# Stage 2 of a long convolution: two frequencies on the partition halves, real and imaginary parts side by side

## The chip, the cores and the metric

One core of a Trainium2 chip runs the whole program in one launch. The metric is device time in microseconds (us), as a median over several executions. The engines are TensorE (PE, with its weight loads shown apart as PEld), VectorE (DVE), ScalarE (ACT), GpSimd (POOL) and SyncE (SP), which here only issues DMAs.

## The reference: a filter convolution, then a feed-forward layer

```python
h_mlp = np.maximum(pos_emb @ w1, 0.0) @ w2            # 12480 x 128
h_filt = h_mlp * np.exp(-0.01 * pos)[:, None]
u = x * v                                             # 2 x 12480 x 128
y = irfft(rfft(u, n=2*S) * rfft(h_filt, n=2*S), n=2*S)[:, :S]
a = x * y                                             # then, per token:
h = a @ w_in                                          # 128 -> 2048
out = (h / (1.0 + np.exp(-h))) @ w_out                # 2048 -> 128
```

The two batches are convolved with the same filter, channel by channel. `w_in` and `w_out` are float64 and are converted on the chip.

## The kernel before, in words

A sequence is padded to two blocks (`NI = 2`) of 6272 = 98 x 64 positions. The long transform is done in two steps, both as matmuls with constant matrices: 98 points along t1 (stage 1), and for each of the 98 results k1 another 64 points along t2, with the twiddle factors folded into the matrix (stage 2). The pointwise product of the spectra is done block by block: the first block of the output is u0*h0, the second u0*h1 + u1*h0.

Stage 1 (lines 213 to 412) is written out by hand in the string `P["seq"]`, one letter a step: `x` loads a group of four channels of x and v, `m` and `d` multiply them on GpSimd and VectorE, `A`/`a` transform a group of batch 0 and copy it out of PSUM on ACT or DVE (`stage_a`, 32 groups), `p` loads positions, `Z` makes 8 of 128 columns of the filter's hidden layer (`zeros_block`, 16 times), `H`/`h` transforms a group of four hidden units (16 groups), and `w` is one step of the conversion of a 512-column piece of `w_in` or `w_out` (8 pieces). In `stage_a` the stationary operand is 98 x 128 (both blocks, 64 positions t2 each) and 196 columns are moved (98 real, 98 imaginary), so that the PSUM rows are (block, t2), while the tile `X` wants (real or imaginary, t2) on its rows; four copies of 64 rows a group do that. Batch 0 comes first here, mixed with the filter's `Z` and the weights; the filter's `H` steps stand behind the `|`.

Stage 2 for batch 0 is the loop at line 536: one iteration takes a pair q of k1 (49 pairs). On PE it issues `up` (transform of X, L419), `sp` (second layer of the filter, L555 and L556, on 64 and 128 rows by turns), `hp` (filter transform three pairs ahead, L290) and `wp` (inverse transform two pairs back, L419). Real and imaginary parts lie on the partition halves there, so that a complex product needs copies across halves: `uw` is i times `up` (two ACT copies, L436, L438), `hab` needs both halves twice (two ACT copies, a DMA from one half to the other at L559, a DVE copy at L575), and `zt` takes four copies (L300 to L303 on ACT for odd pairs, L305 to L308 on DVE for even ones). The products are `at` on DVE and `bt` on POOL (L444, L451), their sum on DVE (L457), and the last addition, `pair_v` (L461), on POOL. Each pair loads one `fb` tile (constants), stores `hs` (the filter's spectrum, used again for batch 1) and `wd` (the result).

Stage 3 is the feed-forward layer over 52 token tiles, with the inverse transform along t1 (`yp`, L611) ahead of each tile, and batch 1 carried through stages 1 and 2 in its shadow. It uses the old `stage_a` and the old pair functions and keeps them.

Each engine works through its queue strictly in the order of the program. SP issues the loads and stores in that order, too.

Of the kernel before, what the change touches and what calls it, by code (L numbers as in the profile page):

```python
# [58 lines left out]
def tile_offsets():  # L59
# [8 lines left out]
    late=2,  # L68
    xb=8,
    pb=4,  # L70
    nw1=6,
    wb1=2,
    wb2=1,
    by1=5,
    by2=9,
    seq='wwppwZxwmxZcwmxxxmmwZwxAAmmpZxxapAxAdwwwAxxwxxAZmZAwddwmpmZwwwwxAmaxwwwwxwawxZxwmwAmAddwAwwZmwAxxxdpxwwmmwwAZmawxwaAwwZwAxwdpwxwwwZmwaAxpwwmwawZmwxxxmwwwwxwwdwwwwAwAwwmwZwwZwwwwwwwwwwwwwAawwwwwwwwwwwwmwZAwwwwwwwwAwawwwwww|HwwhwwHwHwhwwxHwhHHhHHxwwhwwwHwHmhmwfffwwwwwwwwwwAwwwAbwbwwwwbw',
# [13 lines left out]
def kernel(  # L90
# [12 lines left out]
    fb: bass.AP,  # L103
    win: bass.AP,
# [13 lines left out]
    hs = dram.tile([NQ, 64, 1024], F32, name="hs")  # L118
# [3 lines left out]
    fa_sb = const.tile([R, 196], F32, name="fa_sb")  # L122
# [4 lines left out]
    w2_sb = const.tile([128, D], F32, name="w2_sb")  # L127

    def weights(wp, src, nm, bufs, dst):
# [15 lines left out]
        t = wp.tile([128, n], U32, name=f"wt{nm}", tag="wt", bufs=bufs)  # L145
        e = wp.tile([128, n], U32, name=f"we{nm}", tag="we", bufs=bufs)
# [27 lines left out]
        nc.sync.dma_start(out=dst, in_=a)  # L174
# [7 lines left out]
    def skewed(gens, by):  # L182

        live = list(enumerate(gens))
        t = 0
        while live:
            for i, g in list(live):
                if t >= by * i:
                    try:
                        next(g)  # L190
                    except StopIteration:
                        live.remove((i, g))
                        continue
# [9 lines left out]
    NLATE = P["late"]  # L203
    xpool = pool("xpool")
    X = xpool.tile([128, R, NI * D], F32, name="X")
    zpool = pool("zpool")
    z = zpool.tile([R, NJ, 128], F32, name="z")
    stg = pool("stg", side="right")
    wprep = pool("wprep", side="right")
    psz = pool("psz", space=PSUM, side="right")  # L210
    psa = pool("psa", space=PSUM)

    def stage_a(psp, lhs, dst, on_act, nm, bufs):

        ap = psp.tile([128, 4, 256], F32, name=f"ap{nm}", tag="ap", bufs=bufs)
        for k in range(4):
            nc.tensor.matmul(ap[:, k, 0:196], lhs(k), fa_sb, start=True, stop=True)  # L217
# [15 lines left out]
    def uv_tiles(b, g, sp):  # L233
        if b == 1:
            return [slot(512 * k)[0:R].rearrange("p (d t) -> p d t", t=128) for k in (g % 4, 4 + g % 4)]
        n = P["xb"] if g < D // 4 - NLATE else NLATE
        return [sp.tile([R, 4, 128], F32, name=f"{t}s{b}_{g}", tag=t, bufs=n) for t in "xv"]
# [31 lines left out]
    def stage_a_group(b, g, psp, us, bufs, on_act):  # L269
        stage_a(  # L270
# [8 lines left out]
    def load_fb(rp, q, bufs, e):  # L279
        t = rp.tile([128, 2, 2, 128], F32, name=f"fb{q}", tag="fb", bufs=bufs)  # L280
        e.dma_start(out=t, in_=fb[q])
        return t
# [3 lines left out]
    def hb_step(q):  # L286

        hp = php.tile([128, 2, 2, 64], F32, name=f"hp{q}", tag="hp", bufs=2)
        for k in range(2):
            nc.tensor.matmul(  # L290
                hp[:, k].rearrange("p c k -> p (c k)"),
                Xh[2 * q >= KA][:, 2 * q - (2 * q >= KA) * KA + k],
                fbs[q][:, k, 0],
                start=True,
                stop=True,
            )
        zt = rpa.tile([128, 2, 4, 64], F32, name=f"zt{q}", tag="zt", bufs=3)
        hf = hp.rearrange("p k c m -> p (k c) m")
        if q % 2:
            nc.scalar.copy(out=zt[64:128, 1], in_=hf[64:128])  # L300
            nc.scalar.copy(out=zt[0:64, 0], in_=hf[0:64])
            nc.scalar.copy(out=zt[0:64, 1, 1:3], in_=hf[0:64, 0:4:3])
            nc.scalar.activation(out=zt[0:64, 1, 0:4:3], in_=hf[0:64, 1:3], func=AF.Copy, scale=-1.0)  # L303
        else:
            nc.vector.tensor_copy(zt[64:128, 1], hf[64:128])  # L305
            nc.vector.tensor_copy(zt[0:64, 0], hf[0:64])
            nc.vector.tensor_copy(zt[0:64, 1, 1:3], hf[0:64, 0:4:3])
            nc.vector.tensor_scalar(  # L308
                out=zt[0:64, 1, 0:4:3], in0=hf[0:64, 1:3], scalar1=-1.0, scalar2=None, op0=ALU.mult
            )  # L310
        zs[q] = zt
# [5 lines left out]
    nc.scalar.dma_start(out=w2_sb[0:64], in_=w2)  # L317
    nc.scalar.dma_start(out=w2_sb[64:128], in_=w2)
    nc.scalar.dma_start(out=fai_sb, in_=fai)

    def w_gen(k):
# [5 lines left out]
        return weights(wprep, src, k, P["wb1"] if k < P["nw1"] else P["wb2"], dst)  # L327
# [15 lines left out]
    def filter_group(g, on_act):  # L343
        stage_a(
            psa,
            lambda k: z[:, 4 * g + k],
            lambda c, i: [
                (h[64 * c : 64 * c + 64, :, i * NJ + 4 * g : i * NJ + 4 * g + 4], k0, k1)
# [4 lines left out]
            3,  # L353
        )
# [3 lines left out]
    w_steps = skewed([w_gen(k) for k in range(P["nw1"])], P["by1"])  # L358
    n_a = n_z = n_h = n_f = 0
    for t in P["seq"]:  # L360
# [6 lines left out]
        elif t in "Aa":  # L367
            stage_a_group(0, n_a, psa, uss.pop(n_a), 3, t == "A")
            n_a += 1
        elif t == "p":  # L370
            g = len(pts)
            pts.append(wprep.tile([128, NP, R], F32, name=f"pt{g}", tag="pt", bufs=P["pb"]))
# [3 lines left out]
        elif t == "Z":  # L376
            zeros_block(n_z)
            n_z += 1
        elif t in "Hh":
# [556 lines left out]
```

## Time and profile before

| | us |
|---|---|
| median of 3 runs (all: 1633.18, 1633.42, 1628.67) | 1633.18 |
| the profiled execution | 1626.7 |
| its span | 1624.7 |
| PE busy in the span | 1591.1 |
| DVE busy | 1285.6 |
| ACT busy | 1108.2 |
| POOL busy | 575.4 |

The profiled execution's time is 2.0 us over its span, which is what lies around it. Stage 1 fills about the first 116 us, stage 2 the next 186, and stage 3 the rest. The share of busy time is a mean over these, so the stages are looked at one by one. A matmul of f32 operands is shown as two passes, each with a weight load.

### The profile page before, as it was taken

To read this page: it belongs to the slowest core of one execution; us is meant where nothing else is said; L and a number is where in the kernel's file an instruction comes from. 1 tells how busy PE (TensorE), PEld (TensorE's weight loads), DVE (VectorE), ACT (ScalarE), POOL (GpSimd) and SP (SyncE) were. 2 spreads that over 40 slices of the span, in tenths; PEclk is the share of its full clock that TensorE was granted. 3 is DMA by queue.
4 is the path that set the end of the run, shared out by engine and by line. 5 is a ranking of instruction groups with operands and counts; after the bars stand their busy time and mean duration, and the time that the engine had idled before them with its cause. 6 is when DMAs were issued, how large, how long until landed. Compare 5 with 4: busy or idle time off the path is not lost.

```text
span 1624.7 us, 27176 instructions
## 1 busy us (share of the span) xinstructions
PE 1591.1 (98%) x9376; PEld 1369.7 (84%) x9376; DVE 1285.6 (79%) x2182; ACT 1108.2 (68%) x2151; POOL 575.4 (35%) x564
## 2 busy tenths in 40 slices
PE   7899999899999999999999999999999999999999
PEld 6787777688888888988888888888888898888888
DVE  5979899765688889888888887777777777777776
ACT  5598898767777777777777775555555555555555
POOL 5627778632156656666666650000000000000000
PEclk9899999889999999999999999999999999999999
DMA  9838999854255554555554541111111111111110
GB/s 264 235 100 229 237 262 259 236 137 121 77 132 138 132 145 128 153 134 148 135 137 133 135 109 53 43 50 49 33 47 48 47 43 38 44 50 47 35 41 18
DMA packets 130001, 186.99 MB, mean 115 GB/s; under 512 B 11346, under 2 KB 79608, under 8 KB 129864
## 3 DMA queue, kind: packets, MB, share of 16 engines
q1 hardware_dynamic: 89480, 147.58, 33.2%
q10 hardware_dynamic: 40384, 37.67, 8.3%
q8 instruction: 75, 1.23, 0.3%
q14 instruction: 62, 0.51, 0.1%
HBM read 125.36 MB, written 53.42 MB: 110 GB/s over the span
## 4 chain that ended last, share of the span: by engine, by line
PE 79%; DMA 1%; issue 0%; SPq 0%; POOL 0%; ACT 0%; DVE 0%; POOLq 0%
PE op L841 12%; PE op L843 11%; PE op L842 11%; PE hq L814 11%; PE hq L813 11%; PE hq L815 11%; PE yp L611 6%; PE wp L419 2%; PE up L419 2%; PE ap L217 2%; DMA slots<-in_v_dram 1%; DMA slots<-wd 0%; POOL slots L245 0%; SPq L240 0%; DVE att L622 0%
## 5 line engine op out<-in xcount | busy, mean ns | idle before, releaser
L820 ACT ACTIVATE g<-hq 128x486 f32<-128x486 f32 (+3 forms) x448 | 255.6, 570 | 224.2 <-PE hq L815 214.3
L825 DVE TENSOR_TENSOR gl<-g,gh 128x486 fp32r<-128x486 f32 (+3 forms) x448 | 294.4, 657 | 94.7 <-PE hq L815 59.4
L841 PE MATMUL op<-gh,woh 128*128 128x490 f32 (+3 forms) x832 | 323.4, 389 | 0.0
L814 PE MATMUL hq<-al,wih 128*128 128x490 f32 (+3 forms) x832 | 315.9, 380 | 0.0
L813 PE MATMUL hq<-ah,wih 128*128 128x490 f32 (+3 forms) x832 | 315.8, 380 | 0.0
L843 PE MATMUL op<-gh,wol 128*128 128x490 f32 (+3 forms) x832 | 315.4, 379 | 0.0
L815 PE MATMUL hq<-ah,wil 128*128 128x490 f32 (+3 forms) x832 | 315.4, 379 | 0.0
L842 PE MATMUL op<-gl,woh 128*128 128x490 f32 (+3 forms) x832 | 315.1, 379 | 0.0
L820 ACT ACTIVATE hq<-hq 128x490 f32<-128x490 f32 (+2 forms) x384 | 214.1, 559 | 93.8 <-PE hq L815 65.6
L825 DVE TENSOR_TENSOR gl<-hq,gh 128x490 fp32r<-128x490 f32 (+2 forms) x384 | 251.7, 662 | 32.6 <-ACT gh L824 22.1
L822 DVE CAST gh<-hq 128x490 fp32r<-128x490 f32 (+2 forms) x288 | 188.9, 656 | 50.0 <-ACT hq L820 48.4
L822 DVE CAST gh<-g 128x486 fp32r<-128x486 f32 (+3 forms) x336 | 137.7, 410 | 56.9 <-ACT g L820 54.9
L813 PEld LDWEIGHTS hq<-ah,wih 128*128 128x128 f32 x832 | 156.7, 188 | 25.6 <-DVE gl L825 0.8
L814 PEld LDWEIGHTS hq<-al,wih 128*128 128x128 f32 x832 | 156.6, 188 | 24.9
L841 PEld LDWEIGHTS op<-gh,woh 128*128 128x128 f32 x832 | 156.5, 188 | 24.9
L815 PEld LDWEIGHTS hq<-ah,wil 128*128 128x128 f32 x832 | 156.7, 188 | 24.6
L843 PEld LDWEIGHTS op<-gh,wol 128*128 128x128 f32 x832 | 156.3, 188 | 25.0
L842 PEld LDWEIGHTS op<-gl,woh 128*128 128x128 f32 x832 | 156.6, 188 | 19.7 <-DVE gl L825 0.3
L223 ACT COPY X<-ap 64x392 f32<-64x392 f32 x208 | 99.8, 480 | 34.4 <-PE ap L217 32.2
L611 PEld LDWEIGHTS yp<-fai_sb,slots 98*64 98x64 f32 x2048 | 89.3, 138 | 17.9 <-issue 16.7
L611 PE MATMUL yp<-fai_sb,slots 98*64 98x98 f32 (+1 forms) x2048 | 99.4, 252 | 0.3 <-DMA slots<-wd 0.3
L623 ACT CAST ah<-att 128x490 fp32r<-128x490 f32 (+3 forms) x52 | 30.9, 594 | 90.5 <-DVE att L622 90.5
(1068 smaller groups left out, 2546.7 us busy)
## 6 DMA issues: line engine op xcount, KB each, us to landing
slots<-hs SPq DMA_DIRECT2D x98, 256.0 KB
slots<-wd SPq DMA_DIRECT2D x48, 490.0 KB
hs<-hab SPq DMA_DIRECT2D x49, 256.0 KB
wd<-ws SPq DMA_DIRECT2D x49, 256.0 KB
slots<-in_fb_dram SPq DMA_DIRECT2D x49, 256.0 KB
wd<-slots ACTq DMA_DIRECT2D x49, 256.0 KB
fb<-in_fb_dram ACTq DMA_DIRECT2D x45, 256.0 KB
xs<-in_x_dram SPq DMA_DIRECT2D x32, 196.0 KB
```

The lines of the kernel that those rows point to most:

```text
L223: nc.scalar.copy(out=o, in_=src[:, k0:k1])
L419: nc.tensor.matmul(out[:, k].rearrange("p i d -> p (i d)"), f[:, k], a[:, k], start=(i == 0), stop=(i == len(passes) - 1),)
L611: nc.tensor.matmul(yp[h : h + 64, o : o + ws[t]], wt[:, c, t * D + h : t * D + h + 64], fai_sb[:, c, 0 : ws[t]], start=(c == 0), stop=(c = ...
L813: nc.tensor.matmul(hp[:, 0:w], wih[:, fs], ah[:, 0:w], start=True, stop=False)
L814: nc.tensor.matmul(hp[:, 0:w], wih[:, fs], al[:, 0:w], start=False, stop=False)
L815: nc.tensor.matmul(hp[:, 0:w], wil[:, fs], ah[:, 0:w], start=False, stop=True)
L820: nc.scalar.activation(out=g[:, 0:w], in_=hp[:, 0:w], func=AF.Silu)
L822: nc.vector.tensor_copy(gh[:, 0:w], g[:, 0:w])
L825: nc.vector.tensor_tensor(out=gl[:, 0:w], in0=g[:, 0:w], in1=gh[:, 0:w].bitcast(F32), op=ALU.subtract)
L841: nc.tensor.matmul(o[:, 0:w], woh[:, fs], gh[:, 0:w], start=(f == 0), stop=False)
L842: nc.tensor.matmul(o[:, 0:w], woh[:, fs], gl[:, 0:w], start=False, stop=False)
L843: nc.tensor.matmul(o[:, 0:w], wol[:, fs], gh[:, 0:w], start=False, stop=(f == NF - 1))
```

## The change

Stage 2 of batch 0 is laid out anew: the two frequencies of a pair lie on the partition halves, and real and imaginary parts side by side in the free dimension. `up`, `sp` and `hp` become four matmuls each, with 64 stationary columns (column halves of the array: k = 0 to PSUM rows 0 to 63, k = 1 to rows 64 to 127); `wp` becomes four matmuls with 64 rows (row halves), each frequency into a PSUM bank of its own. The constants come in a new array `fc` of the same size. `w2_sb` is block-diagonal. What was a copy across halves is now another place in the same row: `zt` is one copy, `hab` one copy and one negated copy of half the size, `us` one copy. `pair_v` goes to DVE in every iteration.

Stage 1 uses `stage_a_halves` for the filter and for batch 0: 64 stationary columns (one block) and 98 moved ones, real parts to the lower, imaginary ones to the upper half of the PSUM rows, so that two copies of 128 rows a group are left of four of 64. For the filter, the second block also gets the first block's share with another constant, added in PSUM (`wrap`, eight matmuls more a group). The string `seq` is new: all `Z`, then all `H`, then the 32 groups of batch 0. `X` now lies where `z`, the positions and the first four weight pieces were; 14 groups of x and v have a buffer (5 of them in `stg1`, whose room the last four weight pieces take after group 4). Weight stores are issued by GpSimd.

```diff
+    def stage_a_halves(psp, lhs, dst, on_act, nm, bufs, wrap=False):
+        ap = psp.tile([128, NI, 512], F32, name=f"ap{nm}", tag="ap", bufs=bufs)
+        for i in range(NI):
+            for k in range(4):
+                for c in range(2):
+                    nc.tensor.matmul(
+                        ap[64 * c : 64 * c + 64, i, k * R : k * R + R],
+                        lhs(k, i),
+                        fa_sb[:, c * R : c * R + R],
+                        start=True,
+                        stop=not (wrap and i),
+                    )
+                for c in range(2 if wrap and i else 0):
+                    nc.tensor.matmul(
+                        ap[64 * c : 64 * c + 64, i, k * R : k * R + R],
+                        lhs(k, 0),
+                        fa_sb[:, (2 + c) * R : (3 + c) * R],
+                        start=False,
+                        stop=True,
+                    )
+        for i in range(NI):
+            src = ap[:, i, 0 : 4 * R].rearrange("p (d k) -> p k d", d=4)
+            for o, k0, k1 in dst(i):
+                if on_act:
+                    nc.scalar.copy(out=o, in_=src[:, k0:k1])
+                else:
+                    nc.vector.tensor_copy(o, src[:, k0:k1])
...
     def hb_step(q):
...
+            for i in range(NI):
+                nc.tensor.matmul(
+                    hp[64 * i : 64 * i + 64, k],
+                    Xh[2 * q >= KA][:, 2 * q - (2 * q >= KA) * KA + k, i * NJ : i * NJ + NJ],
+                    fbs[q][:, 0, k],
+                    start=True,
+                    stop=True,
+                )
+        zs[q] = rpa.tile([128, 2, 2, 64], F32, name=f"zt{q}", tag="zt", bufs=3)
+        nc.scalar.copy(out=zs[q].rearrange("p k c m -> p k (c m)"), in_=hp)
...
         elif t in "Aa":
+            if n_a == 0:
+                for g in w_steps[: P["nw1"]]:
+                    assert next(g, None) is None
+                wprep.release()
+                ppool.release()
+                zpool.release()
+                xpool = pool("xpool")
+                X = xpool.tile([128, R, NI * D], F32, name="X")
             stage_a_group(0, n_a, psa, uss.pop(n_a), 3, t == "A")
             n_a += 1
+            if n_a == P["x1"]:
+                stg1.release()
+                wprep = pool("wprep2", side="right")
+                w_steps += [w_gen(k) for k in range(P["nw1"], 8)]
...
+    def pair_u0(q):
+        up = pp.tile([128, 2, NI, D], F32, name=f"up0_{q}", tag="up", bufs=2)
+        for c in range(2):
+            for k in range(2):
+                nc.tensor.matmul(
+                    up[64 * k : 64 * k + 64, c].rearrange("p i d -> p (i d)"),
+                    fbs[q][:, 0, k, 64 * c : 64 * c + 64],
+                    X[:, 2 * q + k],
+                    start=True,
+                    stop=True,
+                )
+        us = rp.tile([128, 2, NI, D], F32, name=f"us{q}", tag="uw", bufs=2)
+        nc.scalar.copy(out=us, in_=up)
+        return up, us
+
+    def filter_spectrum(q):
+        sp_ = pps.tile([128, 2, 2, D], F32, name=f"sp{q}", tag="sp", bufs=2)
+        zt = zs.pop(q)
+        for c in range(2):
+            for k in range(2):
+                nc.tensor.matmul(
+                    sp_[64 * k : 64 * k + 64, c].rearrange("p s d -> p (s d)"),
+                    zt[:, k, c],
+                    w2_sb,
+                    start=True,
+                    stop=True,
+                )
+        hab = rp.tile([128, 3, 2, D], F32, name=f"hab{q}", tag="hab", bufs=3)
+        nc.scalar.copy(out=hab[:, 1:3], in_=sp_)
+        nc.scalar.activation(out=hab[:, 0], in_=sp_[:, 1], func=AF.Copy, scale=-1.0)
+        return hab
...
+    def last_w(q):
+        wp = pp.tile([128, 2, 512], F32, name=f"wp0_{q}", tag="wp", bufs=1)
+        at, inv = prods.pop(q)[0], fbs.pop(q)[:, 1]
+        for c in range(2):
+            for k in range(2):
+                h = slice(64 * k, 64 * k + 64)
+                nc.tensor.matmul(wp[:, k, 0:256], inv[h, c], at[h, c], start=(c == 0), stop=(c == 1))
+        store_w(0, q, rp, wp[:, :, 0:256], nb)
...
+        if it >= 0:
+            up, us = pair_u0(it)
+        if it >= 1:
+            pair_s(*prods[it - 1])
+        if it + 1 < NQ:
+            habs[it + 1] = filter_spectrum(it + 1)
+        if 3 <= it + 3 < NQ:
+            hb_step(it + 3)
+        if it >= 0:
+            hab = habs.pop(it)
+            at = products(it, up, hab[:, 1:2], "at", 3, nc.vector)
+            bt = products(it, us[:, ::-1], hab[:, 0:3:2], "bt", 2, nc.gpsimd)
+            prods[it] = at, bt
+            nc.sync.dma_start(out=hs[it], in_=hab[:, 1:3].rearrange("p m s d -> p (m s d)"))
+        if it >= 1:
+            pair_v(prods[it - 1][0], nc.vector)
+        if it >= 2:
+            last_w(it - 2)
         side_steps(it)
```

On PE, one iteration of stage 2 before (here pair 4; sizes are those of the output, x2 or x4 counts like matmuls in a row):

```order
L419 MATMUL up_4_1228<-X,fb_1076 128x256 x2
L555 MATMUL sp_1235<-w_sb,zt_1165 128x128
L556 MATMUL sp_1235<-w_sb,zt_1165 128x128
L555 MATMUL sp_1235<-w_sb,zt_1165 128x128
L556 MATMUL sp_1235<-w_sb,zt_1165 128x128
L290 MATMUL hp_1244<-fb_1185,Xha 128x128 x2
L419 MATMUL wp_2_1261<-at_2_1170,fb_1005 128x256 x2
```

And the same iteration now, with the first of the next:

```order
L551 MATMUL up_4_1792<-X,fb_1644 64x256 x4
L568 MATMUL sp_1800<-w_sb,zt_1731 64x256 x4
L320 MATMUL hp_1808<-fb_1749,Xha 64x128 x4
L601 MATMUL wp_2_1823<-at_2_1733,fb_1533 128x256 x4
L551 MATMUL up_5_1833<-X,fb_1675 64x256 x4
```

The order of the four blocks is the same. The alternation of L555 and L556 is gone; three blocks in a row use column halves, and only `wp` row halves.

On DVE, one iteration of stage 2 with an even pair before:

```order
L305 COPY zt_1288<-hp_1285 64x256
L306 COPY zt_1288<-hp_1285 64x256
L307 COPY zt_1288<-hp_1285 64x128
L308 TENSOR_SCALAR zt_1288<-hp_1285 64x2x64
L444 TENSOR_TENSOR at_5_1293<-up_5_1269,hab_1240 128x512
L451 TENSOR_TENSOR at_5_1293<-up_5_1269,hab_1240 128x256
L575 COPY hab_1281<-hab_1281 64x512
L457 TENSOR_TENSOR at_5_1293<-at_5_1293,bt_5_1296 128x768
```

And every iteration now (the first row is `pair_s` of the pair before, the fourth `pair_v`):

```order
L474 TENSOR_TENSOR at_4_1815<-at_4_1815,bt_4_1818 128x768
L586 TENSOR_TENSOR at_5_1856<-up_5_1833,hab_1805 128x512
L592 TENSOR_TENSOR at_5_1856<-up_5_1833,hab_1805 128x256
L478 TENSOR_TENSOR at_4_1815<-at_4_1815 128x2x128
L474 TENSOR_TENSOR at_5_1856<-at_5_1856,bt_5_1859 128x768
```

The copies of `zt` and `hab` have left DVE, and `pair_v` has come from POOL.

On SP, the middle of stage 1 now (`xs` and `vs` are a group of x and v, `raw` a weight piece):

```order
L260 DMA vs_12_912<-in_v_dram 98x512
L259 DMA xs_13_917<-in_x_dram 98x512
L260 DMA vs_13_918<-in_v_dram 98x512
L133 DMA raw_941<-in_w_out_dram 128x4x256
L133 DMA raw_966<-in_w_out_dram 128x4x256
L259 DMA xs_14_1034<-in_x_dram 98x512
```

Groups 0 to 13 of batch 0 are all issued ahead of the fifth weight piece; the last 18 groups and four weight pieces stand behind it in the queue.

## Rows read from the trace of the kernel before

**Rows 1.** Stretches: us, busy us per engine (count), granted clock, DMA share, GB/s.

```profile
0.00:74.00 74.00, 55.11 (x313) 51.87 (x314) 54.24 (x76) 42.70 (x84) 40.63 (x33) 0.91 0.94 262
74.00:116.00 42.00, 38.93 (x218) 35.74 (x217) 33.43 (x82) 35.29 (x110) 14.30 (x11) 0.96 0.32 100
116.40:302.60 186.20, 184.22 (x949) 142.39 (x948) 168.96 (x288) 163.65 (x340) 145.78 (x144) 1.00 0.87 240
```

**Rows 2.** Timeline of PE in stage 2: start, length, line, operation, count.

```profile
217.26 0.48 PE L555 MATMUL sp<-w_sb,zt 64*128 64x128 f32 x2
...
218.83 0.61 PE L290 MATMUL hp<-fb,Xhb 128*128 128x128 f32 x4
219.28 1.03 PE L419 MATMUL wp<-at,fb 128*128 128x256 f32 x4
220.14 1.03 PE L419 MATMUL up<-X,fb 128*128 128x256 f32 x4
221.10 0.48 PE L555 MATMUL sp<-w_sb,zt 64*128 64x128 f32 x2
```

**Rows 3.** Timeline of PE around one inverse transform in stage 3.

```profile
681.70 1.90 PE L611 MATMUL yp<-fai_sb,slots 98*64 98x97 f32 x40
683.53 0.45 PE L841 MATMUL op<-gh,woh 128*128 128x392 f32 x1
```

**Rows 4.** Line L611, weight loads: count, min/median/max ns, first and last start.

```profile
L611 PEld LDWEIGHTS yp<-fai_sb,slots x2048: 132/136/232, 323.3 to 1591.3; 98*64 98x64 f32 x187
```

**Rows 5.** Chain of waits: start, us, what; one transform of 98x196.

```profile
355.61 1.33 PE ap L217 x8
```

**Rows 6.** Groups by line, DVE in stage 2: count, busy us, mean ns, idle.

```profile
L457 DVE TENSOR_TENSOR at<-at,bt 128x768 f32<-128x768 f32 x47 | 60.5, 1287 | 10.0 <-POOL bt L451 9.3
...
L444 DVE TENSOR_TENSOR at<-up,hab 128x512 f32<-128x512 f32 x47 | 31.8, 677 | 0.8 <-ACT uw L438 0.8
L451 DVE TENSOR_TENSOR at<-up,hab 128x256 f32<-128x256 f32 x47 | 19.2, 408 | 0.0
```

**Rows 7.** Line L461 where DVE runs it.

```profile
L461 DVE TENSOR_TENSOR at<-at x2: 407/416/425, 308.3 to 309.6; 128x256 f32<-128x256 f32 x2
```

**Rows 8.** Groups by line, POOL in stage 2.

```profile
L444 POOL TENSOR_TENSOR bt<-uw,hab 128x512 f32<-128x512 f32 x48 | 70.7, 1472 | 40.9 <-DMA hab<-hab 21.6 <-ACT uw L438 14.6 <-ACT hab L560 2.6
L451 POOL TENSOR_TENSOR bt<-uw,hab 128x256 f32<-128x256 f32 x48 | 40.9, 852 | 0.0
```

**Rows 9.** Groups by line, ACT in stage 2.

```profile
L558 ACT COPY hab<-sp 64x512 f32<-64x512 f32 x49 | 28.5, 581 | 11.2 <-PE sp L556 10.4
...
L473 ACT COPY ws<-wp 128x512 f32<-128x512 f32 x46 | 26.8, 582 | 2.7 <-issue 1.0 <-PE wp L419 0.9 <-ACT hab L560 0.4
```

**Rows 10.** DMA issues from 150 to 300 us: count, KB each.

```profile
hs<-hab SPq DMA_DIRECT2D x39, 256.0 KB
wd<-ws SPq DMA_DIRECT2D x39, 256.0 KB
fb<-in_fb_dram ACTq DMA_DIRECT2D x36, 256.0 KB
hab<-hab SPq DMA_DIRECT2D x39, 128.0 KB
```

**Rows 11.** DMA from 4 to 74 us, in all.

```profile
DMA packets 10342, 18.74 MB, mean 268 GB/s; under 512 B 1244, under 2 KB 2861, under 8 KB 10337
```

**Rows 12.** Groups by line, the first 115 us.

```profile
L223 ACT COPY X<-ap 64x392 f32<-64x392 f32 x92 | 44.1, 479 | 17.1 <-PE ap L217 15.9
L245 POOL TENSOR_TENSOR xs<-xs,vs 98x512 f32<-98x512 f32 x24 | 33.4, 1399 | 23.3 <-DMA vs<-in_v_dram 23.2
...
L334 DVE SCALAR_TENSOR_TENSOR z<-zp,win_sb 98x512 f32<-98x512 f32 x16 | 16.3, 1042 | 9.5 <-PE zp L333 9.4
...
L148 DVE TENSOR_SCALAR wa<-raw 128x512 f32<-128x512 f32 x8 | 5.3, 668 | 6.2 <-DMA raw<-in_w_in_dram 5.2 <-DMA raw<-in_w_out_dram 0.8
```

**Rows 13.** Timeline of PE: stage 2's first up.

```profile
116.41 1.03 PE L419 MATMUL up<-X,fb 128*128 128x256 f32 x4
```

More of the change, by code (lines that the diff above doesn't have):

```diff
@@ L173, in weights @@
         yield
-        nc.sync.dma_start(out=dst, in_=a)
+        nc.gpsimd.dma_start(out=dst, in_=a)
     def split(a, hi, lo):
@@ L202 @@
     WC = 512
[L203 to L205 removed]
     zpool = pool("zpool")
     z = zpool.tile([R, NJ, 128], F32, name="z")
+    ppool = pool("ppool")
+    xhb_pool = pool("xhb", side="right")
+    xha_pool = pool("xha", side="right")
+    Xh = [
+        xha_pool.tile([128, KA, NI * NJ], F32, name="Xha"),
+        xhb_pool.tile([128, R - KA, NI * NJ], F32, name="Xhb", tag="xhb"),
+    ]
+    wprep = pool("wprep")
     stg = pool("stg", side="right")
[L209 removed]
+    stg1 = pool("stg1", side="right")
     psz = pool("psz", space=PSUM, side="right")
     psa = pool("psa", space=PSUM)
+    def stage_a_halves(psp, lhs, dst, on_act, nm, bufs, wrap=False):
[25 more added lines that the diff above has]
+                    nc.vector.tensor_copy(o, src[:, k0:k1])
     def stage_a(psp, lhs, dst, on_act, nm, bufs):
@@ L235, in uv_tiles @@
             return [slot(512 * k)[0:R].rearrange("p (d t) -> p d t", t=128) for k in (g % 4, 4 + g % 4)]
-        n = P["xb"] if g < D // 4 - NLATE else NLATE
+        sp, n = (stg1, P["x1"]) if g < P["x1"] else (stg, P["xb"])
         return [sp.tile([R, 4, 128], F32, name=f"{t}s{b}_{g}", tag=t, bufs=n) for t in "xv"]
@@ L286, in hb_step @@
     def hb_step(q):
-        hp = php.tile([128, 2, 2, 64], F32, name=f"hp{q}", tag="hp", bufs=2)
+        hp = php.tile([128, 2, 128], F32, name=f"hp{q}", tag="hp", bufs=2)
         for k in range(2):
[L290 to L311, printed above, removed]
+            for i in range(NI):
[8 more added lines that the diff above has]
+        nc.scalar.copy(out=zs[q].rearrange("p k c m -> p k (c m)"), in_=hp)
     nc.vector.memset(w1_sb, 0.0)
@@ L357 @@
     pts = []
-    w_steps = skewed([w_gen(k) for k in range(P["nw1"])], P["by1"])
+    w_steps = [w_gen(k) for k in range(P["nw1"])]
     n_a = n_z = n_h = n_f = 0
@@ L378 @@
             n_z += 1
+            if n_z == 16:
+                psz.release()
+                php = pool("php", space=PSUM, side="right")
         elif t in "Hh":
@@ L407 @@
             hb_step(len(zs))
-    for _ in w_steps:
-        pass
-    wprep.release()
     stg.release()
@@ L451, in pair_p @@
         e.tensor_tensor(
-            out=t[:, 2].rearrange("p (k d) -> p k d", k=2), in0=u[:, :, 0], in1=hab[:, m, 1], op=ALU.mult
+            out=t[:, 2].rearrange("p (k d) -> p k d", k=2), in0=u[:, :, 0], in1=hab[:, :, m, 1], op=ALU.mult
         )
@@ L472, in store_w @@
         ws = p.tile([128, 2, NI, D], F32, name=f"ws{b}_{q}", tag=tag, bufs=n)
-        nc.scalar.copy(out=ws, in_=wp)
+        nc.scalar.copy(out=ws.rearrange("p k i d -> p k (i d)"), in_=wp)
         (nc.scalar if b else nc.sync).dma_start(out=wd[b][2 * q : 2 * q + 2].rearrange("k i p d -> p k i d"), in_=ws)
@@ L715, in load_h @@
                 nc.sync.dma_start(
-                    out=hab[64 * h : 64 * h + 64].rearrange("p m s k d -> p (m s k d)"),
-                    in_=hs[q],
+                    out=hab[64 * h : 64 * h + 64].rearrange("p k m s d -> p k (m s d)"),
+                    in_=hs[q].rearrange("(k p) n -> p k n", k=2),
                 )
```

171 lines of the change are left out of this document (61 added, 110 removed).

## The prediction

> **What bounds the kernel now.** I read the busy time stretch by stretch first, then the timeline of PE where a stretch is full, then the groups by line of the other engines, then the DMAs.
>
> The stretches show two different machines [rows 1]. In the first 74 us the DMAs are busy 0.94 of the time at 262 GB/s, and PE 55.1 of 74 us: loads set the pace. From 74 to 116 us the DMAs drop to 0.32 and PE is busy 38.9 of 42 us: the filter's transforms, which stand last in the string. So the loads and this PE work follow one another. [...]
>
> A busy PE is not proof, since the ends of matmuls are modelled, so I look at the starts [rows 2]. One iteration runs from 217.26 to 221.10, 3.84 us, and is made of: sp 1.57 (217.26 to 218.83), hp 0.45, wp 0.86, up 0.96. wp and up stream the same columns, so 0.10 of up's stretch is something else. hp has four passes of 128 columns in 0.45; sp's eight passes of 128 should take 0.90 and take 1.57. What sp has and hp has not is the alternation of 64 and 128 stationary rows: three changes inside and one at its end cost 0.67, or 0.17 each, the one at its start 0.10. I read 0.2 us as the price of one change of form, rounded up. Stage 2 is bound by PE, and about 0.8 us of each 3.84 are changes.
>
> **Stage 2, part by part.** The columns streamed are what they were, as long as two halves of the array work side by side. For column halves the trace shows it: the inverse transform in stage 3 puts 40 passes of 98 columns on 64-column halves between 681.70 and 683.53, 1.83 us [rows 3]; full-width passes of 196 columns take 1.33 for eight [rows 5], which is 0.083 for 98, and 40 of these one after another would take 3.3 us. Twenty pairs at 0.083 are 1.66 and leave 0.17 for the change of form.
>
> New iteration on PE: up 0.86 (eight half passes of 256), sp 0.86 (eight half passes of 256, where eight full ones of 128 stood), hp 0.45, wp 0.86 if the row halves run side by side, and two changes of form (into wp and out of it) at 0.2: 3.43 us. Against 3.84 that is 0.41 less, times 49: 20.1 us. For wp no row of before shows two row halves at once. Its bounds: 0.86 (as the column halves do) and 1.72 (eight passes of 256 columns at 0.215 one after another). I take 0.86, by the nearest row [rows 3]. The changes may cost from 0.10 each, the least seen, so the PE sum may come out at 3.23.
>
> [...]
>
> What is next if PE takes 3.43? DVE per pair: L457 1.287, L444 0.677, L451 0.408 [rows 6], and pair_v, which DVE does in 0.416 [rows 7]: 2.79 us. It loses L575 and half of the zt copies. POOL: 1.472 + 0.852 = 2.32 [rows 8], and loses the wait for the DMA between halves, 21.6 us in all. ACT: a copy of 64 rows x 512 takes 0.581 and one of 128 x 512 takes 0.582 [rows 9], so time goes with the length of a row and not with the rows; three copies of 512 (us, hab, ws) and two of 256 (zt, negated hab), the latter bounded by 0.582 each, are at most 2.9. DMAs: 0.87 of 3.80 is 3.31 us per pair now, for 256 + 256 + 256 + 128 KB [rows 10]. The 128 KB go. By bytes 2.84 are left. By pieces nothing is saved, since hs becomes 128 rows of 2 KB where it was 64 of 4 KB: 3.31. Both are under 3.43, the second only just. So the copies taken off ACT and DVE gain nothing by themselves; PE hides them, and PE stays the bound. The new pair_v on DVE is hidden by the same cover. wp has one buffer instead of two: its copy ws is in the ACT queue right behind it, 0.58, and the next wp is 2.6 us away, behind up, sp and hp.
>
> **Stage 1.** By PE the filter gets dearer: 24 matmuls of two passes a group, 48 half passes, at 0.0415 (pairs at 0.083) 2.0 us, against 1.33 for eight full passes; 16 groups: 32 us. A batch group is 32 half passes, 1.33, as before. The copies of X are halved: 479 ns for a row of 392 [rows 12], two a group and not four. They cost 64 x 0.479 = 31 us less of ACT and DVE time, on engines that were not the bound in the first 74 us, so I count nothing for it there.
>
> The new order: the 16 zero blocks wait for DVE, 1.042 each, and three weight steps of 0.668 stand between them [rows 12]: 18.7 us. I let them start at 7 us (a choice: 1.2 MB at 268 GB/s [rows 11] are 4.5 us, and 2.5 until the first lands). Filter transforms 32 us: 57.7. Five batch groups at 1.33: 64.4. Only then is the room of stg1 free, and the fifth weight piece, which SP issues ahead of group 14, can start; all groups behind it in SP's queue wait with it. Until there the DMAs have had 3.2 MB of positions, four weight pieces with their stores (3.1 MB) and 14 groups (5.6 MB): 12 MB, 45 us at 268 GB/s. They lie idle for some 15 us. From 64.4 on, 18 groups (7.2 MB) and four pieces with stores (3.1 MB) take 38.6 us: 103. Then 2 us to land, a product on POOL 1.40 [rows 12], the last group 1.33, its two copies 0.96, and sp: first up at 110, where it was 116.4 [rows 13]. Gain 6 us. If the DMAs had no hole, PE would still need 7 + 18.7 + 32 + 42.6 and 3 more, 103: a gain of 13. [...]
>
> The edge from stage 2 to 3, and stage 3 itself, keep their instructions; the loads of hs there move the same bytes.
>
> **Sum.** The profiled execution is 1626.7 us. Less 20 in stage 2 and 6 in stage 1: 1600.7. The three runs have a median of 1633.2, 6.5 over the profiled execution; the same 26 off that is 1607. I say 1604, between the two.
>
> **Rivals**, their times counted from the profiled execution.
>
> 1. Row halves one after another. wp takes 1.72, an iteration 4.29, 0.45 more than now: +22 in stage 2, -6 in stage 1, 1643 us: slower. It decides from 1.27 us for a wp on (0.86 + 0.41). For it: nothing in the trace shows row halves at once. Against: column halves do it with the same kind of passes, and each frequency writes its own bank.
>
> [...]
>
> 3. Something else holds stage 2 near 3.7 us: DMAs at 3.31 by pieces have hardly any slack, or the chain ACT us, POOL bt, DVE sum, wp. 49 x 0.14 = 7 less, and 6 in stage 1: 1614. Against: every engine has 0.5 us to spare by rows 6 to 9.
>
> 4. Weight loads of column halves don't hide. A load takes 0.136 us [rows 4]; one bare load a pair of halves is 12 x 0.136 = 1.6 us an iteration, +60 over stage 2, and in stage 1 896 pairs, +122: about 1800 us, slower. The trace speaks against it: 40 loads and 40 passes in 1.83 us [rows 3]. [...] The row decides against it.
>
> **How the numbers follow.** Forecast (PE at about 3.4 in stage 2, stage 1 a little shorter) 0.62, with 1592 to 1616 as its own range; rival 1 0.11, rival 2 0.12, rival 3 0.14, rival 4 0.01. The low end 1584 takes 3.23 us in stage 2 (30 us less) and most of the best case in stage 1 (13 less); the high end 1630 holds rivals 2 and 3 with their tails and leaves out 1 and 4. A measurement here can tell about 0.3%, 5 us, from no change. Faster: the forecast and most of rivals 2 and 3, 0.80. Within: 0.06, from their tails. Slower: rivals 1 and 4 and a rest of 2, 0.14.
>
> **What would show it.** In the trace of the changed kernel: iterations of 3.4 us from up to up; wp in 0.86 with both frequencies' passes starting together; sp in about 0.86; no PE waits in stage 2; first up near 110 us, with a dip of the DMAs at about 50 to 64 us, then full; DVE about 2.8 and ACT under 2.9 us per pair. The forecast is wrong if wp takes over 1.27 us, if an iteration is over 3.7, or if the first up comes after 120 us.

## The result and the profile after

| | before | after |
|---|---|---|
| median, us | 1630.93 (4 runs, 1625.46 to 1633.42) | 1602.11 (4 runs, 1601.19 to 1602.71) |
| ratio to before | 1 | 0.9828, 95% interval 0.9808 to 0.9848 |
| span of the profiled execution | 1624.7 | 1600.6 |
| first `up` of stage 2 | 116.4 | 119.2 |
| last `up` of the loop | 302.1 | 280.3 |

By the medians the kernel became 28.8 us shorter. The spans differ by only 24.1 us, mostly since the profiled execution of before (1626.7 us) lies 4.2 us under its median: stage 1 grew by 2.8, the 48 steps from the first to the last `up` shrank by 24.6 (185.7 to 161.1), and the rest lost 2.3, which no run explains. So the total came out 2 us from the forecast, but by errors of opposite sign: stage 2 gave more than the 20 us, and stage 1 cost time instead of giving 6.

Stretch by stretch, in the columns of [rows 1] (stretch, length, busy us of PE, PEld, DVE, ACT and POOL, granted clock, DMA share, GB/s):

```profile
0.00:74.00 74.00, 66.86 (x1282) 64.72 (x1284) 45.52 (x61) 29.97 (x89) 26.16 (x25) 1.00 0.66 207
74.00:119.20 45.20, 33.49 (x676) 32.52 (x673) 32.77 (x37) 14.42 (x33) 26.21 (x23) 0.89 0.77 217
119.20:280.30 161.10, 159.15 (x1507) 106.37 (x1502) 130.35 (x197) 111.98 (x245) 107.18 (x97) 1.00 0.77 238
```

Stage 2 is the third row: PE is still busy 99% of it, while DVE, ACT and POOL have each become about 38 to 52 us shorter. The second row is where stage 1 goes wrong: PE idles for 12 of 45 us, and its mean granted clock is 0.89.

One iteration of stage 2 on PE, to be held against [rows 2]:

```profile
192.10 1.08 PE L551 MATMUL up<-X,fb 128*64 128x256 f32 x8
193.01 1.03 PE L568 MATMUL sp<-w_sb,zt 128*64 128x256 f32 x8
193.88 0.61 PE L320 MATMUL hp<-fb,Xhb 128*64 128x128 f32 x8
194.41 1.14 PE L601 MATMUL wp<-at,fb 64*128 64x256 f32 x8
195.48 1.08 PE L551 MATMUL up<-X,fb 128*64 128x256 f32 x8
```

From start to start: up 0.91, sp 0.87, hp 0.53, wp 1.07, in all 3.38 us where it was 3.84. Blocks that follow a block of the same form take what their columns took before (sp 0.87, and four pairs of passes at the 0.215 us of one pass of `wp` before are 0.86); what stands around `wp` takes 0.10 (hp), 0.21 (wp) and 0.05 (up) more. The row halves work side by side. The block takes 1.07 us, and eight passes of 256 columns one after another at the 0.215 us of before would take 1.72. The timeline cut to the start and to the end of a single `wp` shows the passes in twos:

```profile
194.41 0.49 PE L601 MATMUL wp<-at,fb 64*128 64x256 f32 x2
...
195.17 0.38 PE L601 MATMUL wp<-at,fb 64*128 64x256 f32 x2
```

A pass here is shown 0.376 us long or longer, and the last two together fill 0.38, so they start within about 0.01 us of each other.

The other engines in stage 2, by groups (count, busy us, mean ns of one, idle time and what ended it), where before had [rows 6 to 9]:

```profile
L586 POOL TENSOR_TENSOR bt<-us,hab 128x512 f32<-128x512 f32 x48 | 63.6, 1325 | 63.8 <-ACT us L559 58.7 <-DVE at L474 4.9
L474 DVE TENSOR_TENSOR at<-at,bt 128x768 f32<-128x768 f32 x47 | 49.9, 1061 | 22.8 <-POOL bt L592 22.8
L592 POOL TENSOR_TENSOR bt<-us,hab 128x256 f32<-128x256 f32 x47 | 43.8, 932 | 0.0
L586 DVE TENSOR_TENSOR at<-up,hab 128x512 f32<-128x512 f32 x48 | 33.1, 690 | 11.5 <-ACT us L559 11.2
L478 DVE TENSOR_TENSOR at<-at 128x256 f32<-128x256 f32 x46 | 30.3, 659 | 0.0
L576 ACT COPY hab<-sp 128x512 f32<-128x512 f32 x49 | 28.8, 587 | 10.1 <-PE sp L568 10.1
L592 DVE TENSOR_TENSOR at<-up,hab 128x256 f32<-128x256 f32 x48 | 19.9, 414 | 0.0
```

DVE needs 1.061 + 0.690 + 0.414 + 0.659 = 2.82 us per pair, POOL 2.26, ACT about 2.5 (three copies of 0.587, and 0.390 and 0.378 at L577 and L328). The 21.6 us in which POOL waited for the DMA between halves [rows 8] are gone. POOL now idles for ACT's copy `us`, in time that PE does not wait for: PE's waits in the loop come to 2.0 us in all.

Stage 1, in a stretch with the same columns as above, shows the hole in the loads:

```profile
46.00:62.00 16.00, 16.00 (x386) 16.00 (x384) 6.13 (x10) 6.71 (x26) 6.77 (x6) 1.00 0.06 18
```

The first batch group starts at 57.3 us (57.7 forecast), SP issues the fifth weight piece at 62.9 (64.4), and the DMAs are nearly idle from 46 to 62 (0.06). The last load of `v` is issued at 100.2, so that the loads end near the forecast 103. Up to here the plan held. What follows did not. PE's waits from 57 to 119 us (who waited for whom, us, times, longest), and one of them in the timeline of all engines:

```profile
PE ap L209 <- DVE xs L264: 8.7, 3, 4.0
PE ap L209 <- POOL xs L264: 2.1, 1, 2.1
```

```profile
82.96 6.16 POOL L264 TENSOR_TENSOR xs<-xs,vs 98x512 f32<-98x512 f32 x5
83.17 6.50 DVE L264 TENSOR_TENSOR xs<-xs,vs 98x512 f32<-98x512 f32 x1
...
89.81 2.55 PE L209 MATMUL ap<-fa_sb,xs 98*64 98x98 f32 x28 [3.96 <-DVE xs L264]
```

Five products x*v on GpSimd run back to back for 6.16 us. One product on VectorE, started 0.21 us after the first, takes 6.50 us, until they are through. The shortest such product on VectorE in this kernel takes 0.68. PE waits 3.96 us for it, and SP issues no load between 86.3 and 92.7 us, since no buffer comes free. The first `up` answers to [rows 13]:

```profile
119.24 1.06 PE L551 MATMUL up<-X,fb 128*64 128x256 f32 x8
```

### The profile page after: what moved, and what is told of

Its sections match the earlier page's. It is cut to its first block, busy times and chain, and to the rows that moved or that the text cites. A ratio compares the mean times of both kernels' runs of the same rounds, so it can differ in the third digit from the quotient of the medians.

```text
span 1600.6 us, 30417 instructions
## 1 busy us (share of the span) xinstructions
PE 1569.5 (98%) x11372; PEld 1339.9 (84%) x11372; DVE 1235.3 (77%) x2028; ACT 1023.4 (64%) x1985; POOL 534.2 (33%) x520
## 4 chain that ended last, share of the span: by engine, by line
PE 93%; DVE 3%; DMA 2%; issue 1%; POOL 1%; ACT 0%; SPq 0%; ACTq 0%; POOLq 0%; DVEq 0%
PE op L889 12%; PE hq L862 11%; PE op L891 11%; PE hq L861 11%; PE op L890 11%; PE hq L863 11%; PE yp L659 6%; PE wp L601 3%; PE ap L236 2%; PE up L551 2%; PE wp L436 2%; PE up L436 2%; PE sp L568 2%; PE ap L209 2%; PE aph L209 1%
## 5 line engine op out<-in xcount | busy, mean ns | idle before, releaser
L586 POOL TENSOR_TENSOR bt<-us,hab 128x512 f32<-128x512 f32 x49 | 65.3, 1333 | 64.3 <-ACT us L559 59.2
```

The lines of the kernel that those rows point to most:

```text
L586: e.tensor_tensor(out=t[:, 0:2].rearrange("p c (i d) -> p c i d", i=NI), in0=u, in1=h0.unsqueeze(2).broadcast_to([128, 2, NI, D]), op=ALU. ...
```

## Experiments

Theory 1 for stage 1: the time is lost at products that two engines compute at once, and at what stands behind them in VectorE's queue. For stage 2, theory 1 is that PE alone bounds the loop, before and after.

**All later products on VectorE.** In the string, every `m` (product on GpSimd) behind the first batch group became `d` (on VectorE); a piece of it:

```diff
-HHaAAmAamxmdxam4A455444m5AAAxA4xxmxx45d5mmA
+HHaAAdAadxddxad4A455444d5AAAxA4xxdxx45d5ddA
```

> All 18 GpSimd products of x and v that stand behind the first batch group in the string go to VectorE; GpSimd is left with the weight steps there. [...] Theory 2 (the loads, which end near 103 us, and the depth of the buffers decide): first up within 2 us of 119, total 1600 to 1604. [...]

Measured: 1599.15 us (ratio to before 0.9801, 0.9787 to 0.9814), first `up` at 116.06 and not 119.24. The products (count, minimum/median/maximum ns):

```profile
L264 DVE TENSOR_TENSOR xs<-xs,vs x26: 674/682/1766, 61.0 to 110.2; 98x512 f32<-98x512 f32 x26
```

The median of VectorE's products fell from 1.75 us to 0.68 and the longest from 6.50 to 1.77; PE's waits fell from 12.0 to 6.0 us, 5.0 of them for products. Theory 1 had put the first `up` at 110 to 113 us and the total at 1594 to 1597. The direction is theory 1's, the size (3 us) about half of what it expected.

**All later products on GpSimd.** The opposite edit, `d` to `m`.

> The reverse: the 8 VectorE products behind the first batch group go to GpSimd. Theory 1: no product can starve, VectorE's weight steps still can, and its copies of X behind them; GpSimd has 26 products of 1.3 us and the weight steps, 43 us in a phase of about 50; first up at 112 to 116 us, total 1596 to 1600. Theory 2: first up within 2 us of 119, total 1600 to 1604.

Measured: 1603.39 us (0.9828, 0.9814 to 0.9841), first `up` at 120.59. The longest of PE's waits, 10.3 us in all:

```profile
PE ap L209 <- POOL xs L264: 5.8, 3, 3.3
```

A miss: taking the products off VectorE removes the overlap too, but at 1.28 us apiece, with weight steps between them, GpSimd's own pace becomes the wait. So the two runs together don't show that the overlap alone is what costs: the first edit also gave GpSimd's products to the engine that does one in 0.68 us.

**Products on VectorE and all copies of X on ScalarE.** The first edit, and every `a` of the batch phase became `A`:

```diff
-HHaAAdAadxddxad4A455444d5AAAxA4xxdxx45d5ddAx544x5aa
+HHAAAdAAdxddxAd4A455444d5AAAxA4xxdxx45d5ddAx544x5AA
```

> Stage 1 as in the run with all later products on VectorE, and besides all X copies of the batch groups go to ScalarE, so that VectorE's queue holds only products and the weight steps. Theory 1 (stage 1 of the changed kernel loses its time at products that VectorE and GpSimd run at the same time, and at copies queued behind them): the first up comes at 110 to 114 us instead of 116.1, TensorE waits less on DVE between 74 and 115 us, total 1594 to 1598. Theory 2 (VectorE's products were the small part; GpSimd's weight steps and ScalarE's own weight steps hold the copies just as long): first up at 115 to 118, total 1598 to 1602.

Measured: 1596.1 us (0.979, 0.9775 to 0.9805), first `up` at 113.12, as theory 1 had it. PE's waits from 57 to 117 us:

```profile
PE ap L209 <- ACT raw L148: 2.2, 1, 2.2
PE ap L209 <- DVE xs L264: 1.4, 3, 0.7
PE ap L209 <- issue: 1.3, 1, 1.3
```

Three us more than the first edit gave, 6.1 in all. This version is faster than both kernels: 6 us under the changed one.

**Stage 1 of before with stage 2 of the change.** The string, buffers and weight steps of before, and `stage_a` for the batch groups; the filter's groups in halves, as the new `zt` needs them.

A piece of the edit:

```diff
-    w_steps = [w_gen(k) for k in range(P["nw1"])]
+    w_steps = skewed([w_gen(k) for k in range(P["nw1"])], P["by1"])
...
-        sp, n = (stg1, P["x1"]) if g < P["x1"] else (stg, P["xb"])
+        n = P["xb"] if g < D // 4 - NLATE else NLATE
```

> Stage 1 in the order of before (batch groups first, filter groups between and behind them) but with the filter groups in halves, which the new layout of z needs; stage 2 as in the changed kernel. It tells what the new order of stage 1 is worth by itself. Theory 1 (the new order is worth about what the filter groups in halves cost): 32 filter groups of 2.0 us instead of 1.33 lie partly on the TensorE-bound end of stage 1, first up at 122 to 126, total 1604 to 1610. Theory 2 (filter groups hide behind the loads in either order): first up at 116 to 118, total 1598 to 1601, and the new order is what costs the 2.8 us.

Measured: 1611.84 us (0.9887, 0.9871 to 0.9904). The first `up`, and the matmuls of the filter's groups (count, minimum/median/maximum ns, first and last start), in the kernel before and then here:

```profile
129.92 1.03 PE L569 MATMUL up<-X,fb 128*64 128x256 f32 x8
```

```profile
L217 PE MATMUL aph<-fa_sb,z x128: 329/329/433, 83.9 to 107.7; 98*128 98x196 f32 x128
```

```profile
L225 PE MATMUL aph<-fa_sb,z x512: 247/248/298, 90.1 to 122.2; 98*64 98x98 f32 x171
```

Stage 2 is the same 161 us. The first `up` comes 13.5 us later than before, more than either theory said. In the old order the filter's groups stand last. In halves they last about 8 us longer (32.1 against 23.8 us from first to last start), and they also start 6.2 us later, which no run explains. The changed kernel's stage 1 is 10.7 us ahead of this one (129.92 to 119.24). That is the worth of its new order together with its batch groups in halves, its buffers and its weight steps, since this run takes all of these back at once. So stage 1's +2.8 is the sum of a cost of 13.5 and a gain of 10.7, with what stands behind each of the two not taken apart further.

**Before, with sp's matmuls grouped.** Two matmuls of 64 rows, then two of 128, in the kernel before:

```diff
             for k in range(2):
                 nc.tensor.matmul(sp_[:, 0, k], zt[0:64, 0, k], w2_sb[0:64], start=True, stop=True)
+            for k in range(2):
                 nc.tensor.matmul(sp_[:, 1, k], zt[:, 1, k], w2_sb, start=True, stop=True)
```

> The kernel before, with sp's two matmuls of 64 rows first and its two of 128 rows behind them, so that two of the four changes of form in an iteration are gone; the copies on ACT and VectorE stay. Theory PE (PE alone bounds stage 2 of before, a change costs 0.17 to 0.2 us): sp from 1.57 to about 1.2, an iteration from 3.84 to 3.45 to 3.5, total 17 to 20 us less. Rival (VectorE with 3.7 us a pair and ACT are next, so that the copies that the change takes away were needed for its gain): an iteration at 3.7 to 3.75, total 4 to 7 us less.

Measured: 1630.5 us, ratio 1.0002 (0.999 to 1.0013). PE's timeline in three iterations, the loop's stretch and the waits in it:

```profile
139.06 1.03 PE L419 MATMUL up<-X,fb 128*128 128x256 f32 x4
...
142.51 0.81 PE L419 MATMUL up<-X,fb 128*128 128x256 f32 x3
...
217.16 0.71 PE L555 MATMUL sp<-w_sb,zt 64*128 64x128 f32 x4
...
218.34 0.61 PE L290 MATMUL hp<-fb,Xhb 128*128 128x128 f32 x4
...
221.02 0.71 PE L555 MATMUL sp<-w_sb,zt 64*128 64x128 f32 x4
...
249.07 1.03 PE L419 MATMUL up<-X,fb 128*128 128x256 f32 x4
...
252.22 1.13 PE L419 MATMUL wp<-at,fb 128*128 128x256 f32 x4 [0.39 <-POOL at L461]
253.65 1.10 PE L419 MATMUL up<-X,fb 128*128 128x256 f32 x4 [0.30 <-DVE at L451]
```

```profile
116.40:302.60 186.20, 175.26 (x936) 136.38 (x936) 174.01 (x283) 161.13 (x338) 139.40 (x139) 0.98 0.89 238
```

```profile
POOL at L461 <- DVE at L457: 20.7, 17, 1.8
...
PE wp L419 <- POOL at L461: 7.0, 10, 1.9
```

sp fell from 1.57 us to 1.18 (217.16 to 218.34) with two changes of form fewer, 0.2 each. An iteration in which PE waits for nothing now takes 3.45 us (139.06 to 142.51), as theory PE said. But others take longer, the one at 217 us 3.86 and the one at 249 us 4.58 (249.07 to 253.65), and from the first `up` (118.12) to the last (307.89) the mean is 3.95, where before had 3.87. In the stretch of [rows 1] PE's busy time fell by 9 us and its idle time rose by as much; what else sp gave up went into later starts behind it (from hp to the next sp 2.68 us, where [rows 2] has 2.27). The waits name a reason: `wp` waits for `pair_v` on POOL, which waits for the sum on DVE, and DVE is busy 174 of 186 us. So the loop of before had two bounds at about the same height. That the second is DVE with this chain is read from the waits; no run frees them alone.

**The loop's `pair_v` on GpSimd.** In the changed kernel:

```diff
-            pair_v(prods[it - 1][0], nc.vector)
+            pair_v(prods[it - 1][0], nc.gpsimd)
```

> The changed kernel with the pair_v sum of the stage 2 loop on GpSimd instead of VectorE. Theory 1 (TensorE alone bounds the new loop, the vector engines have room): iteration stays 3.38 us, total 1600 to 1604. Theory 2 (the loop is held by the chain of products as in the kernel before): GpSimd's three operations reach about 3.2 us a pair, wp waits for them, iteration 3.5 to 3.7 us and total 1608 to 1618.

Measured: 1603.8 us (0.9842, 0.9825 to 0.986). The loop:

```profile
120.00:280.00 160.00, 157.13 (x1488) 104.68 (x1484) 117.34 (x148) 110.39 (x242) 148.40 (x142) 1.00 0.80 239
```

POOL is now busy 93% of the loop, DVE 73%, and `up` still follows `up` after 3.38 us; from the first `up` to the last the loop takes 162.6 us, 1.5 more. The new loop is PE's.

**wp's frequencies in turn.** The two loops of `last_w` exchanged, so that both passes of one frequency stand together:

```diff
-        for c in range(2):
-            for k in range(2):
+        for k in range(2):
+            for c in range(2):
```

> In wp the loop over the frequency becomes the outer one, so that two matmuls on the same row half follow each other; the same matmuls otherwise. Theory A (row halves run side by side only if neighbours in the queue use different halves, and PE bounds stage 2): wp from 1.07 to about 1.7 to 1.9 us, an iteration from 3.38 to 4.0 to 4.25, total 1632 to 1645, which is also the price of the rival in which row halves run one after another. Theory B (PE pairs passes from further back in its queue): wp stays at 1.07, total 1602. Theory C (stage 2 has another bound close by): the iteration grows by less than wp does.

Measured: 1603.05 us (0.9829, 0.9811 to 0.9847). `wp` to `up` is 1.07 us as before:

```profile
194.97 1.14 PE L601 MATMUL wp<-at,fb 64*128 64x256 f32 x8
196.04 1.08 PE L551 MATMUL up<-X,fb 128*64 128x256 f32 x8
```

The halves run side by side in this order too (1.07 us, where eight passes one after another would take 1.72). So the statement above that each engine works strictly in the order of the program, which holds for PE's blocks as the timelines show them, is too strict for its passes here; how PE pairs them no run shows. A serial `wp`, and so rival 1's price, was never seen.

**Two wp in a row.** Half of the changes of form fall away if `wp` is done twice every second iteration.

```diff
+        if it >= 2 and it % 2:
+            last_w(it - 2, pps, "wpb")
         if it >= 0:
             up, us = pair_u0(it)
...
-        if it >= 2:
-            last_w(it - 2)
+        if it >= 2 and it % 2 == 0:
+            last_w(it - 2, pp, "wp")
```

> The changed kernel with two wp blocks (column and row halves) back to back every second iteration, one of them in a PSUM tile of its own for which sp and hp have one buffer instead of two: half of the entries into row halves fall away. Theory 1 (wp takes 1.07 us and not 0.86 because of the change of form, and TensorE bounds the loop): 0.1 to 0.2 us less per iteration, about 3.25 us, stage 2 shorter by 5 to 9 us, total 1593 to 1598. Theory 2 (the 1.07 is inside the block, by how the passes of the halves share the engine, or the one buffer of sp and hp adds a wait): iteration 3.38 us or more, total 1600 to 1612.

Measured: 1652.0 us, slower than before (1.014, 1.0115 to 1.0165). A miss of both theories, by a wait that the edit added:

```profile
199.49 2.08 PE L601 MATMUL wp<-at,fb 64*128 64x256 f32 x8 [1.83 <-DVE at L478]
```

The second `wp` stands one block ahead of where its sum is ready; PE waits some 1.8 us every second iteration, and in the loop its mean granted clock drops to 0.93. It says nothing on the price of a change. So it was tried with `wp` of the pairs two and three behind, on the faster stage 1:

```diff
-        if it >= 2:
-            last_w(it - 2)
+        if it >= 3 and it % 2:
+            last_w(it - 3, pp, "wp")
+            last_w(it - 2, pps, "wpb")
```

> On the stage 1 with all later products on VectorE and all X copies on ScalarE. Two wp blocks back to back at the end of every second iteration, of the pairs two and three behind, so that the second no longer comes a step before its pair_v sum (as it did in the run with two wp in a row, where TensorE waited 1.8 us for it); at has four buffers, fb eight, sp and hp one each. Theory 1 (a change into row halves and out of it costs 0.1 to 0.2 us, and TensorE bounds the loop): two iterations take 6.55 to 6.65 us instead of 6.76, stage 2 is 3 to 5 us shorter, total 1591 to 1594 against 1596.1. Theory 2 (wp's 1.07 us is a property of the block itself): two iterations take 6.7 to 6.8 us, total 1595 to 1598. If one buffer of sp or hp adds a wait, both iterations show it as idle time ahead of sp or hp.

> The same stage 1, with one buffer of sp and hp and nothing else changed: the control for the run with two wp blocks back to back. If the second buffers of sp and hp are idle room, the iteration stays at 3.38 us and the total at 1595 to 1597; if not, TensorE shows idle time ahead of sp or hp and the total is 1600 or more.

Measured: 1597.8 us (0.9801, 0.9774 to 0.9827), and for the control 1595.93 (0.9792, 0.9767 to 0.9817). The control shows that one buffer of sp and hp is enough. With two `wp` in a row, two iterations in which PE waits for nothing and, further on, one in which it waits:

```profile
186.47 1.08 PE L551 MATMUL up<-X,fb 128*64 128x256 f32 x8
...
188.68 1.03 PE L551 MATMUL up<-X,fb 128*64 128x256 f32 x8
...
190.94 2.00 PE L601 MATMUL wp<-at,fb 64*128 64x256 f32 x16
192.87 1.08 PE L551 MATMUL up<-X,fb 128*64 128x256 f32 x8
...
197.78 0.66 PE L320 MATMUL hp<-fb,Xhb 128*64 128x128 f32 x8 [0.80 <-DMA fb<-in_fc_dram]
```

Two `wp` take 1.93 us (190.94 to 192.87), 2 x 0.86 and 0.21 once: the 0.21 belongs to the change and not to the block, as theory 1 says. Two undisturbed iterations take 6.40 us (186.47 to 192.87) instead of 6.76, so one whole way into row halves and out, 0.36, has fallen away. But the total is in theory 2's range, and the mean from first to last `up` is 3.40 us a pair and 3.38 in the control: PE gives the gain back in waits, most of them for the load of `fb`. PE's longest wait in the loop (us in all, times, longest), in the control and then here:

```profile
PE hp L320 <- DMA fb<-in_fc_dram: 1.3, 2, 0.8
```

```profile
PE hp L320 <- DMA fb<-in_fc_dram: 7.6, 7, 1.9
```

DVE's sum became dearer as well; in the control and then here:

```profile
L474 DVE TENSOR_TENSOR at<-at,bt 128x768 f32<-128x768 f32 x38 | 37.4, 984 | 18.6 <-POOL bt L592 18.6
```

```profile
L474 DVE TENSOR_TENSOR at<-at,bt 128x768 f32<-128x768 f32 x38 | 56.9, 1498 | 9.3 <-POOL bt L592 9.3
```

The timeline of this loop shows why: where POOL's product starts just ahead of the sum, the sum takes 2.06 us, and 0.94 or 0.95 where POOL is idle.

```profile
196.90 1.26 POOL L586 TENSOR_TENSOR bt<-us,hab 128x512 f32<-128x512 f32 x1
196.93 2.06 DVE L474 TENSOR_TENSOR at<-at,bt 128x768 f32<-128x768 f32 x1 [0.62 <-POOL bt L592]
```

PE's waits tell the two apart: besides the 7.6 us for `fb` it waits only once for DVE, 2.2 us (1.2 in the control). So the late loads take most of the some 8 us that 23 times 0.36 had to give; why the loads are late stays open.

## Why the prediction was right, and where it was not

**PE's new iteration: right.** 3.43 was forecast, 3.38 came. The parts too: column halves 0.87 (0.86), hp and the way into `wp` 0.53, row halves and the way out 1.07 (0.86 + 0.2). The price of a change read from [rows 2], 0.2 us, was confirmed twice: by the grouped sp in the kernel before (0.39 for two), and by two `wp` in a row (0.36 for one way in and out).

**"Stage 2 is bound by PE": not by PE alone.** A PE that was busy 184.2 of 186.2 us [rows 1] looked like the only bound. Taking 0.39 us an iteration off PE alone gained nothing (ratio 1.0002), since by the waits DVE and the chain sum, `pair_v`, `wp` stood at about the same height. So the copies that left ACT and DVE, of which the prediction said that they "gain nothing by themselves", were needed for PE's gain to show; what they are worth with PE as it was, no run tells. With 3.80 us a pair (186.2 us over 49 pairs) and DVE at 169 of 186 us in [rows 1], DVE's slack was no more than 0.35 us a pair, less than the 0.41 to be saved: the row was there to be read. The forecast did not suffer, because the change frees both. For a change that frees only PE the same sum would have been wrong: 49 x 0.39 is 19 us, and the run that did this gained none of it.

**Stage 2's size: 24.6 us, not 20.** The middle iteration gained 0.46 (3.84 to 3.38); over 48 steps that is 22.1. Of the other 2.5, 1.4 are iterations of before that were longer than the one read (185.7 / 48 is 3.87), and 1.1 are shorter ones after it (161.1 / 48 is 3.36; its first iterations have no `wp` yet, and its last no hp). One iteration was taken for the mean.

**Other engines: right in sum.** DVE 2.82 against 2.79, but made up otherwise: `pair_v` 0.659 where 0.416 was read from a place without a GpSimd product beside it [rows 7], the sum 1.061 where [rows 6] has 1.287. DMAs 0.77 of 3.36, 2.6 us a pair, under both ends that were given (2.84 and 3.31). No cover was missing, as `pair_v` on GpSimd showed from the other side.

**Stage 1: the failed step is the tail, "2 us to land, a product on POOL 1.40, the last group 1.33, its two copies 0.96, and sp: first up at 110".** All up to the end of the loads came within about 2 us. But the term took one product for all: the products came in bursts, on two engines at once, one held up to 6.50 us, in a VectorE queue that also had copies and weight steps. No run shows the 2 us to land by themselves: the last load of `v` is issued at 100.2 us, and the last products start at 106.9 on VectorE and 108.0 on GpSimd. From the end of the loads to the first `up` it took 16 us and not 7. Part of that is the clock: PE's mean granted clock was 0.89 between 74 and 119 us, with readings of 0.50 from 87 to 93 us and from 111 to 113, and of 1.00 in most of the rest. By these two levels it was at 0.50 for some 22% of that time, an estimate. The stage's passes start at 12.7 a us between 89.8 and 93.1 us, and at 24 a us between 99.8 and 105.0. Moving the products and the copies gave 6.1 of the 9.2 us back, so most of the loss lay in who does them and in what order. How much of it was two engines computing products at once, and how much GpSimd's slower product, was not taken apart: with all products on GpSimd the overlap was gone too, and nothing was gained. The last 3 stay open; PE still waits 5.1 us there (2.2 for a weight step on ACT, 1.4 for products on DVE), and its granted clock from 74 to 115 us is 0.92. With 119.2 us the first `up` came just short of the 120 at which the prediction called itself wrong.

**The total: near by luck.** Between the two profiled executions 26 us were forecast and 24.3 came. The terms were off by more than that: stage 2 gave 4.6 too much, stage 1 8.8 too little, and the rest 2.3 that no term had. And 1604 was taken between two baselines 6.5 us apart.

**Rivals.** Rival 1 and 4 did not come: both kinds of halves run at once (sp 0.87, `wp` 1.07), with their weight loads hidden (in the loop PE is busy 159.15 of 161.10 us, with 106.37 us of loads beside it). Rival 2, a loss of 10 us in stage 1 and a total of 1617, came in part: the hole was as long as forecast, and the loads ended when the sum said; the loss was behind it, +2.8. The +10, which the high end of the forecast's range holds too, was the author's estimate, and no run shows it. Rival 3 did not come, but it is next: with 0.18 us a pair less on PE the loop no longer followed, and PE waited for `fb` loads.

**What two engines do to each other.** The trace of the changed kernel has a VectorE product of two SBUF operands at 6.50 us (the shortest: 0.68) beside five GpSimd products, and the run with two ready `wp` a sum at 2.06 us, not 0.94, beside one. The product ended 0.55 us after the last of the five, which ran for 6.16 us together; the sum ended 0.83 us after the GpSimd product of 1.26 us that had started 0.03 us ahead of it. Both look as if they had been held until then and had done their own work behind it, the product over five instructions in a row. That is read from the times; no run takes it apart. VectorE's `at<-up,hab`, which reads one operand from PSUM, kept its time beside GpSimd's products, which mostly ran during it. In stage 2 of the changed kernel (count, minimum/median/maximum ns), `at<-up,hab` with `up` in PSUM, and `pair_v` with both operands in SBUF:

```profile
L586 DVE TENSOR_TENSOR at<-up,hab x48: 677/692/693, 121.0 to 279.7; 128x512 f32<-128x512 f32 x48
```

```profile
L478 DVE TENSOR_TENSOR at<-at x46: 409/664/1322, 124.9 to 277.6; 128x256 f32<-128x256 f32 x46
```

## What to carry to other kernels

An engine that is busy 99% need not be the only bound (here 0.39 us an iteration off PE alone left the ratio at 1.0002): compare the second-busiest engine's slack per iteration with what is to be saved, and where the slack is smaller, expect the gain only from a change that frees both. When work is moved between phases, count not only loads and TensorE but the queues of VectorE and GpSimd in the new phase, and look there for operations of both engines with two SBUF operands at the same time, where something waits for the result (here 6.50 us for a product of 0.68, and 2.06 for a sum of 0.94). A change of the array's form was paid here per change and not per matmul (0.36 us for the way in and out, with one `wp` inside or two), so blocks of one form may be put together, but only as far as the operands are ready: it took 0.36 us off PE every two iterations, and late loads took it back.

## What was not expected of the hardware

- Two row halves of one block ran side by side also when the program had two matmuls of one half and then two of the other: 1.07 us either way.
- A change between column halves and row halves cost about 0.36 us for the way in and out (0.10 + 0.21 + 0.05), whether one or two blocks stand inside: with two blocks, two iterations took 6.40 us and not 6.76.
- A VectorE product was held for 6.50 us, over five GpSimd products of 6.16 us together, and not just until the end of the one that ran when it started. In the loop a sum of 2.06 us did get its turn behind the first of two products.
- VectorE's `at<-up,hab`, with one operand in PSUM, was not slowed by GpSimd's products beside it (0.677 to 0.693 us); `pair_v`, with both in SBUF, was (0.409 to 1.322 us).
